# The two full attention layers of a four-layer kernel: scores issued in runs of three pairs, value products behind them, and the operands of the next quad loaded across block borders

## The chip, the cores and the metric

The kernel runs on one core of one Trainium2 chip. The metric is the device time of one execution in microseconds. Before the change it is 2768.49 us (median of three runs, 2767.56 to 2770.2).

## The reference

Four attention layers follow one another on x of 2048 rows by 512 columns (one batch): a window layer (each query sees itself and the 255 keys before it), a full layer, a window layer and a full layer. Each has 32 heads of 16 columns.

```python
x = x + _A_ref(_layernorm(x), A_wqkv, A_wo)      # window layer
x = x + _B_ref(_layernorm(x), B_wqkv, B_wo)      # full layer
x = x + _A_ref(_layernorm(x), A_wqkv, A_wo)
x = x + _B_ref(_layernorm(x), B_wqkv, B_wo)

def _B_ref(x, wqkv, wo):                         # B, S, D = 1, 2048, 512; H = 32; Dh = 16
    qkv = (x @ wqkv).reshape(B, S, 3, H, Dh).transpose(2, 0, 3, 1, 4)
    q, k, v = qkv[0], qkv[1], qkv[2]
    p = softmax(einsum("bhqd,bhkd->bhqk", q, k) * Dh ** -0.5)     # no mask: all 2048 keys
    o = einsum("bhqk,bhkd->bhqd", p, v)
    return o.transpose(0, 2, 1, 3).reshape(B, S, D) @ wo
```

The change is about the two calls of `_B_ref`, layers 1 and 3 (counted from 0).

## The kernel before, in words

**Units of the full layers.** The 2048 queries are cut into four blocks c of 512, the heads into eight quads qd of four, the keys into sixteen tiles j of 128. Layer 1 goes through c, then qd, then j. Layer 3 goes through t (pairs of quads), then c, then the two quads of t, then j. Each layer so has 32 quads in all, 512 key tiles and 1024 *pairs*: a pair is two heads of one key tile.

**A pair** (`exps`, L706 to L719): TensorE makes two score products of 128 keys by 512 queries (L714) into one score tile, and ScalarE takes the exponential of the whole tile, 128 by 1024 (L718), into a buffer e. There are three score tiles in a full layer: two of the pool `ps_s` (L198) and a third one made by `phase` (L408). They are used in turn (L709), so the scores of pair p overwrite what the exponential of pair p-3 reads. There are six e buffers (`EB`, L34).

**The values of a key tile** (`pv` in `attn_full`, L756 to L760): four products of 17 value columns, one for each head, added up in `acc[0]` over the sixteen tiles. They read the two e buffers of the tile. When a quad is done, `epilogue` (L678) has VectorE move `acc[0]` out and divide by the sums; the values of the next quad go to the same `acc[0]`.

**Side work.** Projections, output products and normalisation of other blocks and layers are generators (`Work`, L799). In full layers they hand out one *piece* at a time: four matmuls of 32 output columns over 512 (or 256) columns (`mms`, L427 to L430), which the program counts as 0.222 us (`MM`, L32). Twelve pieces make a group in most of them, three in `wo_part`. All groups of a full layer are added up in the one bank `acc[1]` (L412 to L413), which must be read out before the next group starts; `mms` notes the time from which that is so in `PH["free"]` (L438). `Side` (L860) doles the pieces out: `step` (L908) is called once for each key tile, `share` (L924) gives out pieces by a budget, and `finish` (L935) issues all that is left. In layer 1 there are two `Side` objects (the first half of block 0, then the rest of the layer), in layer 3 one for each of the sixteen blocks (t, c).

**Order.** TensorE's order is that of the program as written (`manual_schedule`, L203); a planned clock (`clock`, `spent`) only decides which side work is handed out where. In `attention` (L955), for each key tile of a full layer: scores of both pairs, then the values of the tile two before (`flush(2)`, L984), then side work (`sd.step()`, L985). So TensorE's order is S S V X, S S V X, with S the scores of a pair, V the values of a key tile, and X side work of zero to several pieces.

**Operands.** `load_full` (L727) loads the queries of a quad (two buffers) and its keys in two halves (three buffers) over SyncE's DMA queue. `attention` calls it for the next quad of the same block at the start of a quad (L977), and for the first quad of a block at the start of the block (L972), behind `sd.finish()` and `settle()` of the block before (L991 and L993). `settle` (L587) issues the small products that are still open after key and query projections.

Of the kernel before, what the change touches and what calls it, by code (L numbers as in the profile page):

```python
# [19 lines left out]
P = 128  # L20
NT = S // P
# [165 lines left out]
def fast_path(ctx, tc, flag, a_x, a_wqkv, a_wo, b_wqkv, b_wo, out):  # L187
# [25 lines left out]
    def spent(us):  # L213
        clock[0] += us
        return us
# [161 lines left out]
    def share(ty):  # L377

        s = vp.tile([P, NHT], F32, name=f"sh{ty}", tag="sh")
        h = vp.tile([P, NHT], F32, name=f"sg{ty}", tag="sh")  # L380
        q, k = (es[:, ty, i, :].bitcast(I32) for i in (0, 1))
        s, h = s.bitcast(I32), h.bitcast(I32)
        nc.vector.tensor_scalar(s, q, 1, None, op0=ALU.logical_shift_right)
        nc.vector.tensor_scalar(h, k, 1, None, op0=ALU.logical_shift_right)
        nc.vector.tensor_tensor(s, s, h, ALU.add)
        nc.vector.tensor_scalar(k, s, 0x7F800000, None, op0=ALU.bitwise_and)
        nc.vector.tensor_tensor(s, s, k, ALU.subtract)
        nc.vector.tensor_tensor(h, s, s, ALU.add)
        nc.vector.tensor_tensor(q, k, h, ALU.add)
# [197 lines left out]
    def settle(all_=True):  # L587
        while pend and (all_ or pend[0][0] <= clock[0]):
            pend.pop(0)[1]()
# [116 lines left out]
    def exps(name, kt, qt, pr, pieces):  # L706

        turn["s"] += 1
        ps = PH["third"] if PH["full"] and turn["s"] % 3 == 0 else ps_s.tile([P, 2, QC], F32, name=f"s{name}", tag="s")  # L709
        w0 = min(p[3] for p in pieces)  # L710
        w1 = max(p[3] + p[2] for p in pieces)
        for kc, qc, wd_, s0 in pieces:
            for h in range(2):
                nc.tensor.matmul(ps[:, h, s0:s0 + wd_], kt[R * h:R * h + R, pr, kc:kc + P],  # L714
                                 qt[R * h:R * h + R, pr, qc:qc + wd_], start=True, stop=True)
        spent(0.27)
        e = pp.tile([P, 2, QC], F32, name=f"e{name}", tag="e", bufs=EB)
        nc.scalar.activation(e[:, :, w0:w1], ps[:, :, w0:w1], AF.Exp, scale=SCALE)  # L718
        return e  # L719

    def flush(n):
        while len(pvq) > n:
            spent(1.0)
            for f in pvq.popleft():
                f()
# [21 lines left out]
            nc.sync.dma_start(kt[:, :, :WIN], kw[c - 1][pair, :, QC - WIN:].rearrange("r p n -> p r n"))  # L747
        return kt, qt

    def attn_full(l, c, qd, kt, qt, a):  # L750
        for j in range(NT):
            es_ = []
            for pr in range(2):
                es_.append(exps(f"{l}_{c}_{qd}_{j}_{pr}", kt[j // 8], qt, pr, [(j % 8 * P, 0, QC, 0)]))

            def pv(j=j, es_=es_):  # L756
                for h in range(4):
                    nc.tensor.matmul(a[32 * h:32 * h + DH + 1, :], V[l, qd // 4, j // 8][:, j % 8, 4 * (qd % 4) + h, :],  # L758
                                     es_[h // 2][:, h % 2, :], start=(j == 0), stop=(j == NT - 1),
                                     skip_group_check=True)  # L760
            yield pv

# [95 lines left out]
    class Side:  # L860

        def __init__(self, steps, works=(), following=(), least=0.0):
            self.next, self.least = list(following), least
            self.q, self.steps, self.cost, self.spent, self.k = [], steps, 0.0, 0.0, 0
            self.budget = self.lag = 0.0
            for w in carried:
                self.add(w)
            carried.clear()
            for w in works:
                self.add(w)  # L870
# [5 lines left out]
        def one(self, force=False):  # L876

            if force:
                self.prefetch()
            at = [(w.ready_at(), i) for i, w in enumerate(self.q)]  # L880
            at = [(r, i) for r, i in at if r is not None]
            now = [i for r, i in at if r <= clock[0]]
            if now:
                i = now[0]
            elif force:
                r, i = min(at)
                clock[0] = r
            else:
                return None
            return self.piece(self.q[i])  # L890

        def piece(self, w):
            c = w.advance()
            if c is None:
                self.q.remove(w)
                return 0.0
            self.spent += abs(c)
            return c

        def prefetch(self):  # L900
# [4 lines left out]
                if any(w.w and not w.open for w in part):  # L905
                    break

        def step(self):  # L908
            self.k += 1
            self.prefetch()  # L910

            for w in list(self.q):
                r = w.ready_at() if w.aside else None
                if r is not None and r <= clock[0]:
                    self.piece(w)
            if PH["full"]:
                return self.share()
            s0, due = self.spent, self.cost * self.k / (self.steps - 2)
            while self.q and self.spent < due and self.spent - s0 < 3:
                c = self.one()  # L920
                if c is None or c < 0 and self.spent - s0 >= 2 and due - self.spent < 4:
                    break

        def share(self):  # L924

            self.budget = min(self.budget + max((self.cost - self.spent) / max(self.steps - 3 - self.k, 1), self.least), 0.75)
            self.lag = max(self.lag - max(0.29, self.least), -0.3)
            while self.q and clock[0] >= PH["free"] and self.budget >= MM / 2 and (self.lag < 0.25 or self.budget > 0.45):
                c = self.one()
                if c is None:  # L930
                    break
                self.budget -= abs(c)
                self.lag += abs(c)

        def finish(self):  # L935

# [7 lines left out]
    def run(g):  # L944
        for _ in g:
            pass
# [5 lines left out]
    pvq = deque()  # L952
    PK, PV, PO = 48 * MM + 0.3, 48 * MM, 48 * MM

    def attention(l, works):  # L955

        win = l % 2 == 0
        phase(l)
        load = load_win if win else load_full
        sd = None  # L960
        for t in range(NHT if l == 3 else 1):
            for c in range(NQ):
                qds = range(2 * t, 2 * t + 2) if l == 3 else range(NQD)
                if l == 1:

                    sd = sd or Side(NT * NQD // 2, works[0], works[1], 0.33)
                    while ("Q", 1, c) not in DONE:
                        sd.one(True)
                    settle()
                else:  # L970
                    sd = Side((3 if win else NT) * len(qds), works[t * NQ + c], works[t * NQ + c + 1], 0.34 if l == 3 and t < 2 else 0.0)
                ops = load(l, c, qds[0])  # L972
                for qd in qds:
                    if (l, c, qd) == (1, 0, NQD // 2):
                        sd.finish()
                        sd = Side(NT * NQD * NQ - NT * NQD // 2, works[1], works[2], 0.33)
                    nxt = load(l, c, qd + 1) if qd + 1 in qds else None  # L977
                    a = acc[qd % 2 if win else 0]
                    began = clock[0]
                    for f in (attn_win if win else attn_full)(l, c, qd, *ops, a):  # L980
                        clock[0] = max(clock[0], began + (2.4 if win else 1.8))
                        began = clock[0]
                        pvq.append([f])
                        flush(2)  # L984
                        sd.step()  # L985
                        if win:
                            settle(False)
                    pvq[-1].append(lambda l=l, c=c, qd=qd, a=a: epilogue(l, c, qd, a))
                    ops = nxt
                if l != 1 or c == NQ - 1:  # L990
                    sd.finish()  # L991
                if not win:
                    settle()  # L993
        flush(0)
        phase(None)

    def T(l, c):
# [15 lines left out]
    def shift3(ht):  # L1013
        def gen():
            key_shift(3, ht)
            yield -1e-6
        return Work(gen(), 0.0, None, [("K3", c, ht) for c in range(NQ)])

    def O3(c, ht):
        return Work(wo_part(c, ht), PO / 4, None, [("O", 3, c, ht)], True)  # L1020
# [21 lines left out]
    def all_of(works, following=()):  # L1042
        Side(1, works, following).finish()
# [102 lines left out]
    lasts = {0: [VV(1, 3)], 2: [VV(3, 3, True, (0,))]}  # L1146
    for l in range(4):
        if l % 2 == 0:
            attention(l, works[l] + [tails[l]])
            all_of(tails[l], lasts[l])  # L1150
            key_shift(l + 1, 0 if l else None)
            all_of(lasts[l], works[l + 1][0])
        else:
            attention(l, works[l] + [works[2][0] if l == 1 else [O3(3, 3)]])
    all_of([O3(3, 3)])


# [37 lines left out]
```

## Time and profile before

| what | us |
|---|---|
| median of three runs | 2768.49 |
| profiled execution | 2767.5 |
| its span, first to last instruction | 2765.8 |
| TensorE matmul busy | 2629.3 |
| ScalarE busy | 2377.9 |
| VectorE busy | 959.7 |
| GpSimd busy | 567.7 |

The profiled execution took 2767.5 us, of which 2765.8 us lie between its first and its last instruction. Busy times are sums over the whole span; the stages have different limits, so they are to be read stage by stage. Layer 1 takes about the stretch from 507 to 1458 us, layer 3 that from 1792 to 2748 us of the span. In the profile a line such as "L714 PE MATMUL s<-qt,kt" is TensorE's score product, "L758" the value product, "L429" (and L550) side work of the full layers, and "L718 ACT" the exponential. A busy TensorE is not a TensorE at its peak, since matmuls overlap.

### The profile page before, as it was taken

To read this page: it belongs to the slowest core of one execution; us is meant where nothing else is said; L and a number is where in the kernel's file an instruction comes from. 1 tells how busy PE (TensorE), PEld (TensorE's weight loads), DVE (VectorE), ACT (ScalarE), POOL (GpSimd) and SP (SyncE) were. 2 spreads that over 40 slices of the span, in tenths; PEclk is the share of its full clock that TensorE was granted. 3 is DMA by queue.
4 is the path that set the end of the run, shared out by engine and by line. 5 is a ranking of instruction groups with operands and counts; after the bars stand their busy time and mean duration, and the time that the engine had idled before them with its cause. 6 is when DMAs were issued, how large, how long until landed. Compare 5 with 4: busy or idle time off the path is not lost.

```text
span 2765.8 us, 59954 instructions
## 1 busy us (share of the span) xinstructions
PE 2629.3 (95%) x24502; PEld 779.9 (28%) x24502; DVE 959.7 (35%) x2063; ACT 2377.9 (86%) x2683; POOL 567.7 (21%) x1129
## 2 busy tenths in 40 slices
PE   8989989999999999999998888899999999999997
PEld 4333334322222222222223333422222222222221
DVE  7678765112131113112215676512222222222122
ACT  3666655799999999999995677399999999999997
POOL 2577662000000000000005677100000000000000
PEclk9999999999999999999999999999999999999999
DMA  7877775422232123212325564623333343333331
GB/s 225 224 244 227 224 202 161 139 70 89 85 100 88 63 81 108 85 60 91 101 68 177 149 186 133 177 66 112 105 117 116 120 124 104 102 107 114 99 96 56
DMA packets 318542, 345.32 MB, mean 125 GB/s; under 512 B 113072, under 2 KB 234416, under 8 KB 312240
## 3 DMA queue, kind: packets, MB, share of 16 engines
q1 hardware_dynamic: 318256, 341.39, 41.0%
q8 instruction: 194, 3.18, 0.5%
q14 instruction: 92, 0.75, 0.1%
HBM read 228.59 MB, written 96.99 MB: 118 GB/s over the span
## 4 chain that ended last, share of the span: by engine, by line
PE 74%; ACT 8%; issue 6%; DVE 6%; POOL 3%; DMA 3%; SPq 0%; ACTq 0%; DVEq 0%; POOLq 0%
PE acc L758 30%; PE s L714 19%; PE acc L429 10%; PE b L432 9%; ACT e L718 7%; PE acc L791 3%; PE bs L432 1%; POOL e L781 1%; POOL e L784 1%; DVE ot L686 1%; POOL wr L344 1%; DMA w<-wd 1%; DVE xh L469 1%; DVE sp L528 0%; DVE xn L463 0%
## 5 line engine op out<-in xcount | busy, mean ns | idle before, releaser
L718 ACT ACTIVATE e<-s 128x1024 f32<-128x1024 f32 (+2 forms) x2432 | 2245.6, 1115 | 106.4 <-PE s L714 98.4
L758 PE MATMUL acc<-e,vt 128*17 128x512 f32 x8192 | 1078.8, 598 | 4.9 <-DVE ot L686 4.1
L714 PE MATMUL s<-qt,kt 64*128 64x512 f16 (+3 forms) x5504 | 777.8, 355 | 68.2 <-ACT e L718 40.0
L714 PEld LDWEIGHTS <-kt 64*128 64x128 f16 x5504 | 203.1, 94 | 807.4 <-issue 776.0
L784 POOL TENSOR_SCALAR_AFFINE_SELECT e<-e 128x256 f32<-128x256 f32 x512 | 230.4, 457 | 116.0 <-ACT e L718 115.3
L758 PEld LDWEIGHTS acc<-e,vt 128*17 128x17 f32 x8192 | 136.2, 95 | 383.6 <-issue 351.8
L686 DVE STREAM_TRANSPOSE ot<-acc 128x512 f32<-128x512 f32 x128 | 91.3, 714 | 374.6 <-PE acc L758 308.5
L781 POOL TENSOR_SCALAR_AFFINE_SELECT e<-e 128x256 f32<-128x256 f32 x448 | 196.8, 445 | 91.0 <-ACT e L718 89.5
L702 POOL TENSOR_TENSOR oh<-o,oh 128x512 f16<-128x512 f32 x31 | 36.0, 1161 | 860.2 <-DVE oh L701 860.2
L791 PE MATMUL acc<-e,vt 128*17 128x384 f32 (+2 forms) x2816 | 202.0, 393 | 6.1 <-POOL e L781 4.0
L432 PE MATMUL b<-xc,w 128*128 128x512 f16 x684 | 159.4, 384 | 16.8 <-DMA w<-wd 7.8
L533 POOL TENSOR_TENSOR sq_h<-sp_h 128x512 bf16<-128x512 f16 x27 | 28.1, 1041 | 510.8 <-DVE sp_h L527 510.8
L525 ACT ACTIVATE sp<-b,es 128x512 f16<-128x512 f32 x57 | 39.2, 688 | 96.0 <-PE b L432 93.7
L527 DVE TENSOR_SCALAR sp<-acc,es 128x512 f16<-128x512 f32 x28 | 20.9, 748 | 288.9 <-PE acc L429 288.9
L638 DVE COPY vt<-acc 128x256 f32<-128x256 f32 (+1 forms) x40 | 20.2, 504 | 288.9 <-PE acc L429 288.9
L527 DVE TENSOR_SCALAR sp_h<-acc,es 128x512 f16<-128x512 f32 x27 | 20.3, 751 | 277.8 <-PE acc L429 277.1
L533 POOL TENSOR_TENSOR sq<-sp 128x512 bf16<-128x512 f16 x28 | 29.1, 1041 | 396.9 <-DVE sp L527 396.9
L429 PE MATMUL acc<-xc,w_h 128*32 128x512 f16 x1296 | 108.1, 379 | 2.3 <-DVE km L566 2.3
L429 PE MATMUL acc<-xc,w 128*32 128x512 f16 x1344 | 108.9, 379 | 0.3
L673 DVE TENSOR_TENSOR dx<-acc,gcol 128x512 f32<-128x512 f32 x60 | 41.5, 692 | 176.7 <-PE acc L429 176.7
L429 PE MATMUL acc<-wv,xc 128*32 128x256 f16 (+1 forms) x1920 | 101.7, 306 | 0.0
L429 PE MATMUL acc<-wo,oh 128*32 128x512 f16 x1296 | 101.3, 379 | 0.0
(167 smaller groups left out, 1767.0 us busy)
## 6 DMA issues: line engine op xcount, KB each, us to landing
kt<-kf SPq DMA_DIRECT2D x128, 512.0 KB
qt<-qs SPq DMA_DIRECT2D x128, 256.0 KB
xd<-x SPq DMA_DIRECT2D x96, 256.0 KB
x<-xd SPq DMA_DIRECT2D x96, 256.0 KB
w<-wd SPq DMA_DIRECT2D x20, 1024.0 KB
kt<-kw SPq DMA_DIRECT2D x64, 256.0 KB
qs<-sp SPq DMA_DIRECT2D x48, 256.0 KB
wo<-wd SPq DMA_DIRECT2D x12, 1024.0 KB
```

The costliest lines, as they stand in the source:

```text
L429: nc.tensor.matmul(ps[g:g + 32], a[:, g:g + 32], b, start=(i == 0), stop=(i == len(pairs) - 1), skip_group_check=True)
L432: nc.tensor.matmul(ps, a, b, start=(i == 0), stop=(i == len(pairs) - 1))
L527: nc.vector.tensor_scalar(sp[:, 0], ps, e, None, op0=ALU.mult)
L533: nc.gpsimd.tensor_tensor(sq, sp[:, 0], sp[:, 0], ALU.mult)
L673: nc.vector.tensor_tensor(d, ps, gcol[1], ALU.mult)
L686: nc.vector.transpose(ot.rearrange("p b r -> p (b r)"), a)
L714: nc.tensor.matmul(ps[:, h, s0:s0 + wd_], kt[R * h:R * h + R, pr, kc:kc + P], qt[R * h:R * h + R, pr, qc:qc + wd_], start=True, stop=True)
L718: nc.scalar.activation(e[:, :, w0:w1], ps[:, :, w0:w1], AF.Exp, scale=SCALE)
L758: nc.tensor.matmul(a[32 * h:32 * h + DH + 1, :], V[l, qd // 4, j // 8][:, j % 8, 4 * (qd % 4) + h, :], es_[h // 2][:, h % 2, :], start=(j ...
L781: nc.gpsimd.affine_select(v, v, pattern=[[0, 2], [-1, P]], compare_op=ALU.is_gt, fill=0.0, base=0, channel_multiplier=1)
L784: nc.gpsimd.affine_select(v, v, pattern=[[0, 2], [1, P]], compare_op=ALU.is_ge, fill=0.0, base=0, channel_multiplier=-1)
L791: nc.tensor.matmul(a[32 * h:32 * h + DH + 1, q * P:(q + nb) * P], V[l, (4 * c + j) // 4][:, j % 4, 4 * qd + h, :], es_[h // 2][:, h % 2, s ...
```

## The change

In the full layers TensorE's order becomes runs of three pairs: the scores of three pairs (one and a half key tiles, without regard to quad borders), then the values of at most two key tiles that were complete at the end of the run before, then side work. A run in which the output of a quad is finished (`epilogue`) takes no values behind it. `Side.step` gets a `room`: 1.79 us less 0.87 us for each key tile's values in this run, but at least one piece, or two where a quad ends. The old brake `lag` goes; the cap of the budget is six pieces (1.332 us), and the least income is 0.65 us for a run in place of 0.33 or 0.34 us for a key tile. Side work that has begun a group goes on with it (`within`). The operands of the next quad are loaded in the second half of a quad, also over the border of a block, once the works that make them are done; if they are not, they are loaded at the start of the quad as before. The window layers get a function of their own, with the old loop.

```diff
-    def attn_full(l, c, qd, kt, qt, a):
...
+    def values_of(l, c, qd, j, es_):
+
+        def pv():
+            spent(0.87)
+            for h in range(4):
+                nc.tensor.matmul(acc[0][32 * h:32 * h + DH + 1, :], V[l, qd // 4, j // 8][:, j % 8, 4 * (qd % 4) + h, :],
+                                 es_[h // 2][:, h % 2, :], start=(j == 0), stop=(j == NT - 1), skip_group_check=True)
+        return pv
...
+            if self.within and self.within in self.q:
+                return self.piece(self.within)
...
+            self.within = w if PH["full"] and c > 0 else None
             return c
...
-        def share(self):
-
-            self.budget = min(self.budget + max((self.cost - self.spent) / max(self.steps - 3 - self.k, 1), self.least), 0.75)
-            self.lag = max(self.lag - max(0.29, self.least), -0.3)
-            while self.q and clock[0] >= PH["free"] and self.budget >= MM / 2 and (self.lag < 0.25 or self.budget > 0.45):
+        def share(self, room):
+
+            self.budget = min(self.budget + max((self.cost - self.spent) / max(self.steps - 2 - self.k, 1), self.least), 6 * MM)
+            while self.q and clock[0] >= PH["free"] and self.budget >= MM / 2 and room >= MM / 2:
                 c = self.one()
                 if c is None:
                     break
                 self.budget -= abs(c)
-                self.lag += abs(c)
+                room -= abs(c)
...
+    def attention_full(l, works):
...
+        runs = lambda n: n * 2 * NT // 3
+        sd, ops, block = None, None, -1
+        pairs, began, ready, due = 0, clock[0], [], deque()
+
+        def upcoming(i):
+
+            t, c, qd = quads[i]
+            if l == 1:
+                return [("Q", 1, c)]
+            return [("Q3", c, t), ("S3", t)] + [("K3", k, t) for k in range(NQ)]
+
+        def emit(all_=False):
+            n, over = 0, False
+            while due:
+                f = due[0]
+                if f.__name__ == "pv":
+                    if not all_ and (n == 2 or over):
+                        break
+                    n += 1
+                else:
+                    over = True
+                due.popleft()()
+            return n, over
+
+        def run():
+
+            nonlocal pairs, began
+            pairs = 0
+            spent(0.22)
+            n, over = emit()
+            due.extend(ready)
+            ready.clear()
+            sd.step(max(1.79 - 0.87 * n, 2 * MM if over else MM))
+            clock[0] = began = max(clock[0], began + 2.71)
+
+        for i, (t, c, qd) in enumerate(quads):
+            if l == 1 and qd == 0 or l == 3 and qd % 2 == 0:
+                if l == 3:
+                    if sd:
+                        sd.finish()
+                    b = t * NQ + c
+                    sd = Side(runs(2), works[b], works[b + 1], 0.65 if t < 2 else 0.0)
+                else:
+
+                    sd = sd or Side(runs(NQD // 2), works[0], works[1], 0.65)
                     while ("Q", 1, c) not in DONE:
                         sd.one(True)
...
+            elif (l, c, qd) == (1, 0, NQD // 2):
+                sd.finish()
+                sd = Side(runs(NQD * NQ - NQD // 2), works[1], works[2], 0.65)
+            kt, qt = ops or load_full(l, c, qd)
+            ops = None
+            for j in range(NT):
+                es_ = []
+                for pr in range(2):
+                    es_.append(exps(f"{l}_{c}_{qd}_{j}_{pr}", kt[j // 8], qt, pr, [(j % 8 * P, 0, QC, 0)]))
+                    if pr:
+                        ready.append(values_of(l, c, qd, j, es_))
+                        if j == NT - 1:
+                            ready.append(lambda c=c, qd=qd: epilogue(l, c, qd, acc[0]))
+                    pairs += 1
+                    if pairs == 3:
+                        run()
+                        if j >= NT // 2 and not ops and i + 1 < len(quads) and all(d in DONE for d in upcoming(i + 1)):
                             settle(False)
...
+                            if not pend:
+                                ops = load_full(l, *quads[i + 1][1:])
+        due.extend(ready)
+        sd.finish()
+        settle()
+        emit(True)
         phase(None)
```

More of the change, by code (lines that the diff above doesn't have):

```diff
@@ L748, in load_win @@
         return kt, qt
-    def attn_full(l, c, qd, kt, qt, a):
[L751 to L761, printed above, removed]
+    def values_of(l, c, qd, j, es_):
[5 more added lines that the diff above has]
+        return pv
     WTILES = (((-2, 0, 1, 0), (1, 1, 3, 1)), ((-1, 0, 2, 0), (2, 2, 2, 2)), ((0, 0, 3, 0), (3, 3, 1, 3)))
@@ L864, in __init__ @@
             self.q, self.steps, self.cost, self.spent, self.k = [], steps, 0.0, 0.0, 0
-            self.budget = self.lag = 0.0
+            self.budget = 0.0
+            self.within = None
             for w in carried:
@@ L906, in prefetch, with step @@
                     break
-        def step(self):
+        def step(self, room=0.0):
             self.k += 1
@@ L916, in step @@
             if PH["full"]:
-                return self.share()
+                return self.share(room)
             s0, due = self.spent, self.cost * self.k / (self.steps - 2)
@@ L953, in fast_path, with attention_win @@
     PK, PV, PO = 48 * MM + 0.3, 48 * MM, 48 * MM
-    def attention(l, works):
-        win = l % 2 == 0
+    def attention_win(l, works):
         phase(l)
[L959 to L966, printed above, removed]
+        for c in range(NQ):
+            sd = Side(3 * NQD, works[c], works[c + 1])
+            ops = load_win(l, c, 0)
+            for qd in range(NQD):
+                nxt = load_win(l, c, qd + 1) if qd + 1 < NQD else None
+                a = acc[qd % 2]
+                began = clock[0]
+                for f in attn_win(l, c, qd, *ops, a):
+                    clock[0] = max(clock[0], began + 2.4)
+                    began = clock[0]
+                    pvq.append([f])
+                    flush(2)
+                    sd.step()
+                    settle(False)
+                pvq[-1].append(lambda c=c, qd=qd, a=a: epilogue(l, c, qd, a))
+                ops = nxt
+            sd.finish()
+        flush(0)
+        phase(None)
@@ new lines, in attention_full @@
+    def attention_full(l, works):
+        phase(l)
+        quads = [(t, c, qd) for t in range(NHT if l == 3 else 1) for c in range(NQ)
+                 for qd in (range(2 * t, 2 * t + 2) if l == 3 else range(NQD))]
+        runs = lambda n: n * 2 * NT // 3
[36 more added lines that the diff above has]
+                    sd = sd or Side(runs(NQD // 2), works[0], works[1], 0.65)
@@ L967, in attention @@
                     while ("Q", 1, c) not in DONE:
                         sd.one(True)
[L969 to L986, printed above, removed]
-                            settle(False)
-                    pvq[-1].append(lambda l=l, c=c, qd=qd, a=a: epilogue(l, c, qd, a))
-                    ops = nxt
@@ L990, in attention @@
[L990 to L994, printed above, removed]
+                settle()
[16 more added lines that the diff above has]
+                        if j >= NT // 2 and not ops and i + 1 < len(quads) and all(d in DONE for d in upcoming(i + 1)):
+                            settle(False)
+                            if not pend:
+                                ops = load_full(l, *quads[i + 1][1:])
@@ L995, in attention @@
+        due.extend(ready)
+        sd.finish()
+        settle()
+        emit(True)
         phase(None)
@@ L1016, in gen @@
             yield -1e-6
-        return Work(gen(), 0.0, None, [("K3", c, ht) for c in range(NQ)])
+        return Work(gen(), 0.0, ("S3", ht), [("K3", c, ht) for c in range(NQ)])
     def O3(c, ht):
@@ L1148, in fast_path @@
         if l % 2 == 0:
-            attention(l, works[l] + [tails[l]])
+            attention_win(l, works[l] + [tails[l]])
             all_of(tails[l], lasts[l])
             key_shift(l + 1, 0 if l else None)
+            DONE["S3", 0] = clock[0]
             all_of(lasts[l], works[l + 1][0])
         else:
-            attention(l, works[l] + [works[2][0] if l == 1 else [O3(3, 3)]])
+            attention_full(l, works[l] + [works[2][0] if l == 1 else [O3(3, 3)]])
     all_of([O3(3, 3)])
```

## The prediction

> **What bounds the kernel now.** First the page, for the span; then the instructions of layer 1 (507 to 1460 us) and layer 3 (1792 to 2750 us) grouped by line.
>
> ```profile
> span 2765.8 us, 59954 instructions
> PE 2629.3 (95%) x24502; PEld 779.9 (28%) x24502; DVE 959.7 (35%) x2063; ACT 2377.9 (86%) x2683; POOL 567.7 (21%) x1129
> ...
> L718 ACT ACTIVATE e<-s 128x1024 f32<-128x1024 f32 x1024 | 947.1, 1084 | 3.7 <-PE s L714 2.7
> ...
> L718 ACT ACTIVATE e<-s 128x1024 f32<-128x1024 f32 x1024 | 946.7, 1199 | 14.4 <-PE s L714 13.5
> ```
>
> The exponentials fill ScalarE in both layers: 1024 in each, hardly any idle time before them. The timeline gives their pace and the ends of each layer:
>
> ```profile
> 699.22 13.88 ACT L718 ACTIVATE e<-s 128x1024 f32<-128x1024 f32 x15
> 507.05 7.45 ACT L718 ACTIVATE e<-s 128x1024 f32<-128x1024 f32 x8
> 1456.78 1.09 ACT L718 ACTIVATE e<-s 128x1024 f32<-128x1024 f32 x1
> 1792.42 1.02 ACT L718 ACTIVATE e<-s 128x1024 f32<-128x1024 f32 x1 [5.96 <-PE s L714]
> 2745.84 1.71 ACT L718 ACTIVATE e<-s 128x1024 f32<-128x1024 f32 x1
> ```
>
> A single one takes about 1.02 us (fourth row), but fifteen in a row take 13.88, so the next ends (13.88 - 1.04) / 14 = 0.917 us after the one before. At that pace 1024 need 1.02 + 1023 x 0.917 = 939.1 us. Layer 1 takes 507.05 to 1457.87, 950.8 us, and layer 3 takes 1792.42 to 2747.55, 955.1 us. So **ScalarE is the bound, and 11.7 + 16.0 = 28 us is all that any order of TensorE can win in the two layers.**
>
> Where the 28 us go, and TensorE's costs, is read from a stretch of its timeline:
>
> ```profile
> 660.53 0.61 PE L429 MATMUL acc<-xc,w 128*32 128x512 f16 x8
> 661.08 0.61 PE L714 MATMUL s<-qt,kt 64*128 64x512 f16 x4
> 661.62 1.05 PE L758 MATMUL acc<-e,vt 128*17 128x512 f32 x8
> 662.49 0.40 PE L429 MATMUL acc<-xc,w 128*32 128x512 f16 x4
> 662.82 0.61 PE L714 MATMUL s<-qt,kt 64*128 64x512 f16 x4
> ...
> 669.00 1.05 PE L758 MATMUL acc<-e,vt 128*17 128x512 f32 x8
> 669.98 0.39 PE L714 MATMUL s<-qt,kt 64*128 64x512 f16 x2
> ```
>
> From start to start: scores of two pairs to values 0.54; values of a tile to side work 0.87; two pieces (x8) to the next scores 0.55, one piece (x4) 0.33, so 0.22 a piece; values straight to scores 0.98. A key tile with two pieces takes 0.54 + 0.87 + 0.55 = 1.96 us, over ScalarE's 2 x 0.917 = 1.83; with one it takes 1.74. Tiles alternate between one and two, 1.85 on average: TensorE falls behind by a few hundredths for each tile, by 0.12 where two pieces follow two.
>
> **The order and its price.** No product, exponential or DMA is added or removed; only TensorE's order, and the place of the operand loads, change. A run of three pairs needs ScalarE for 3 x 0.917 = 2.75 us. What the run saves: the changes scores-values and side work-scores come 341 times in a layer in place of 512. Each cycle has about 0.10 + 0.11 us of them (0.54 less two pairs at 0.22; 0.33 less 0.22), so 171 x 0.21 = 36 us less TensorE time in each layer. The Trainium skill ("TensorEngine Tiling (Array Packing)", Key Properties) says that changing the tiling mode drains the engine. By that rule alone the new order wins; the rows show the same price of a change (and none from values to side work, 0.87 against 0.86 for values to values), but as time of an engine that is not the bound, and that case is rival (1).
>
> What it adds is **a wait of the third pair's scores.** There are three score tiles used in turn, so pair p cannot be written before the exponential of pair p-3 has ended. In the old order a run of two pairs leaves one tile spare, and in layer 1 the scores waited for ScalarE once:
>
> ```profile
> PE s L714 <- ACT e L718: 0.5, 1, 0.5
> ...
> 507.95 1.04 ACT L718 ACTIVATE e<-s 128x1024 f32<-128x1024 f32 x1
> 508.85 1.06 ACT L718 ACTIVATE e<-s 128x1024 f32<-128x1024 f32 x1
> 509.96 0.39 PE L714 MATMUL s<-qt,kt 64*128 64x512 f16 x2 [0.53 <-ACT e L718]
> 510.28 1.05 PE L758 MATMUL acc<-e,vt 128*17 128x512 f32 x8
> ```
>
> That one case shows the price. The exponential ends at 508.85 + 1.06 = 509.91, the waiting scores start 0.05 later, and the values behind them start at 510.28, 0.32 after the scores, though the exponentials that they read had ended by 507.95 + 1.04 = 508.99: nothing behind a waiting matmul passes it. In a run of three, the third pair waits for the third exponential of the run before. Let that end at E. From E ScalarE has three exponentials left, and the first one after them is on time if it ends by E + 4 x 0.917 = E + 3.67. How long before that its scores must start:
>
> ```profile
> 2006.19 0.61 PE L714 MATMUL s<-qt,kt 64*128 64x512 f16 x4
> 2006.68 1.02 ACT L718 ACTIVATE e<-s 128x1024 f32<-128x1024 f32 x1 [1.42 <-PE s L714]
> ...
> 1458.28 0.33 PEld L758 LDWEIGHTS acc<-e,vt 128*17 128x17 f32 x8
> 1458.49 1.90 PE L758 MATMUL acc<-e,vt 128*17 128x512 f32 x16
> 1458.93 0.12 PEld L758 LDWEIGHTS acc<-e,vt 128*17 128x17 f32 x4 [0.31 <-issue]
> 1459.36 0.12 PEld L758 LDWEIGHTS acc<-e,vt 128*17 128x17 f32 x4 [0.31 <-issue]
> ```
>
> Start of the scores to end of the exponential is 0.49 + 1.02 = 1.51. Values behind values step by 0.43 for half a tile, 0.86 for a tile. So the next run's scores must start by E + 2.16, and before them stand 0.05 + 0.32 and then the run's values and side work: **these may take 1.79 us.** A run with two tiles and one piece takes 0.86 + 0.87 + 0.33 = 2.06: late by 0.27. Without a piece it takes 0.86 + 0.98 = 1.84: late by 0.05. A run with one tile and four pieces takes 0.87 + 3 x 0.22 + 0.33 = 1.86, but behind a late run its third pair no longer waits, so it costs nothing and makes up the rest; then its successor's third pair waits again. The sum of two runs (2 x 0.75 for six pairs, plus 2.06 and 1.86) is 5.42, under ScalarE's 5.50: TensorE has the time, but a wait of some 0.37 in every second run takes it away.
>
> How often: runs and key tiles stand three to two, so one and two tiles alternate. Walking the rule through the code, a layer has 341 runs; a two-tile run begins 160 times behind a shorter one, 150 of these alone and 10 followed by another. A two-tile run gets one piece whenever side work is ready (room one `MM`). Of the 150, 140 cost 0.27, and 10, which end a quad, get two pieces and cost 0.49. In the 10 doubles the end of a quad has put off a key tile's values by a run, and the second exponential waits for the e buffer: the values end at about E + 0.37 + 1.05, the exponential so at E + 2.44 in place of 1.83, 0.61 late, and the second run adds 0.27. That is 37.8 + 4.9 + 8.8 = 51.5 us a layer; some 13 runs in layer 1 and 10 in layer 3 find no side work, less 0.22 each: **98 us in both.** Nearest bounds: 0.05 for all 320, 16 us; 0.27 and more for all, 103.
>
> **Side work that does not fit.** One and four pieces alternate, but a group's end stops the run's pieces (`PH["free"]`), so twelve pieces go as 1, 4, 1, 4, 1, 1: six runs, two pieces a run.
>
> ```profile
> L429 PE MATMUL acc<-xc,w 128*32 128x512 f16 x1344 | 108.9, 379 | 0.3
> L429 PE MATMUL acc<-wv,xc 128*32 128x256 f16 (+1 forms) x1152 | 70.0, 326 | 0.0
> L429 PE MATMUL acc<-wo,oh 128*32 128x512 f16 x576 | 46.4, 379 | 0.0
> ...
> L528 DVE SCALAR_TENSOR_TENSOR sp<-acc,es,sp 128x512 f16<-128x512 f32 x28 | 21.0, 751 | 0.9
> L527 DVE TENSOR_SCALAR sp<-acc,es 128x512 f16<-128x512 f32 x28 | 20.9, 748 | 288.9 <-PE acc L429 288.9
> ...
> 1458.72 0.69 DVE L638 COPY vt<-acc 128x512 f32<-128x512 f32 x1 [7.98 <-PE acc L429]
> ```
>
> Layer 1 has 3072 / 48 = 64 groups: 12 half-width ones in the first `Side`, which fit, and 52 in the second, 312 runs where 299 are; and three times nothing is ready for some 8 runs between an output block and the projections that need its normalisation. Some 7 groups are left for `finish`, with ScalarE idle: three of keys, 12 x 0.22 + two readouts of 0.75 + 0.4 = 4.5 each, four of values, 2.6 + 0.69 + 0.3 = 3.6 each; 28 less a lead of 2: **26 us.** In layer 3 a block of t < 2 has about 26 runs' work in 21: two groups of `wo_part`, some 2.3 us with readouts, are forced at the border, of which 1.8 show, seven times, and about 5 us in the later blocks: **18 us.** Bounds: nothing if the groups fit, and twice these.
>
> **Operands.** The loads keep their number; they stand later in their quad, half a quad (over 13 us) ahead of use, and no longer behind a block's last side work. Layer 3's first load bounds a missed one:
>
> ```profile
> 1787.86 19.10 SPq L735 DMA_DIRECT2D kt<-kf  x2
> 1791.71 1.46 PE L714 MATMUL s<-qt,kt 64*128 64x512 f16 x6 [5.67 <-DMA kt<-kf]
> ```
>
> Scores start 3.9 us after it is issued. I take it as covered; what it can win at borders is in the 28 us, and three missed at the borders of t would cost 12. The window layers' code does the same as before: nothing.
>
> **The sum.** 2767.5 (the profiled execution) - 28 + 98 + 26 + 18 = 2881.5; the median stands 1 us above that execution: **2882 us**, 4% slower.
>
> **Rivals.**
> (1) *TensorE had been the bound, and the spared changes free it*: both layers run at 939 us, 2768 - 28 = 2740. For it: the X8 tiles over 1.83, and the total of 5.42 under 5.50. It needs the third pair's wait not to bind: from values and side work of at most 1.79 in every run on, and two tiles alone take 1.84. 0.09.
> (2) *Two-tile runs seldom get a piece* (the planned clock holds work back): 320 x 0.05 = 16 in place of 98, and 0 to 20 of forced work: 2756 to 2776. 0.09, a third of it on each side of no change.
> (3) *Late runs as worked out, but the side work fits*: 2882 - 44 = 2838. 0.18.
> (4) *TensorE's clock falls*, since it now stops shortly in every second run.
>
> ```profile
> 1700.00:1800.00 100.00, 84.11 (x765) 43.09 (x767) 57.95 (x126) 47.74 (x64) 36.20 (x84) 0.93 0.57 158
> 2300.00:2400.00 100.00, 99.15 (x905) 24.06 (x903) 26.99 (x53) 100.00 (x110) 4.51 (x5) 1.00 0.38 116
> ```
>
> Full layers had a granted clock of 1.00; at 84% busy, between layers, it was 0.93. At 0.93 the 2.38 us before the next scores grow by 0.17, 320 times: 2882 + 54 = 2936. 0.04. The Trainium skill ("TensorE: Matmul & The Clock Gate", A second HAM failure mode: psum-queue depth-cycling) says that short idle spells between groups of matmuls can make the gate swing; no run here shows that at this scale.
>
> The forecast itself has 0.60. Faster by over 0.2% (about what a measurement here can tell from no change): 0.09 + 0.03 = 0.12; within: 0.03; slower: 0.85. The range leaves out (1) and (2): from 2800 (half the two-tile runs late, little forced) to 2940 (more forced, or the clock).
>
> **What would show it.** Scores (L714) waiting for ScalarE (L718) some 170 times in each layer, 50 us or more; in a two-tile run 0.37 + 2.06 us from the third pair's scores to the next run's scores; exponentials idle by about 0.27 once in six; a burst of side work at the end of layer 1. If the scores wait but the exponentials keep their pace, 1.79 is wrong; if they do not wait at all, the argument falls.

## The result and the profile after

| | us |
|---|---|
| before, median of 4 runs | 2768.02 (2766.88 to 2770.2) |
| after, median of 4 runs | 2895.47 (2891.85 to 2899.36) |
| ratio | 1.046, 95% interval 1.044 to 1.0479 |
| profiled execution before, after | 2767.5, 2899.36 |

The change makes the kernel 4.6% slower. The page of the changed kernel gives the same work over a longer span (the value products now stand on line 755):

```profile
span 2897.6 us, 59956 instructions
PE 2618.6 (90%) x24502; PEld 873.2 (30%) x24502; DVE 959.4 (33%) x2063; ACT 2397.6 (83%) x2683; POOL 567.1 (20%) x1129
```

Where the 131.8 us between the two spans came from is read from the first and the last exponential of each full layer in the timeline:

```profile
508.96 1.03 ACT L718 ACTIVATE e<-s 128x1024 f32<-128x1024 f32 x1
1497.65 1.02 ACT L718 ACTIVATE e<-s 128x1024 f32<-128x1024 f32 x1 [0.17 <-PE s L714]
1855.63 1.02 ACT L718 ACTIVATE e<-s 128x1024 f32<-128x1024 f32 x1 [6.54 <-PE s L714]
2877.41 1.02 ACT L718 ACTIVATE e<-s 128x1024 f32<-128x1024 f32 x1
```

| stretch | before | after | more |
|---|---|---|---|
| up to layer 1's first exponential | 507.05 | 508.96 | 1.9 |
| layer 1's exponentials | 950.8 | 989.7 | 38.9 |
| from there to layer 3's first | 334.6 | 357.0 | 22.4 |
| layer 3's exponentials | 955.1 | 1022.8 | 67.7 |
| rest of the span | 18.2 | 19.2 | 1.0 |

Nearly all of it lies in the two layers and right behind layer 1. ScalarE's pace of 939.1 us for a layer is the measure for what follows: layer 1 is now 50.6 us over it (11.7 before), layer 3 is 83.7 over (16.0). I call this the *surplus* of a layer.

The groups and the waits of layer 1, then of layer 3, show what the exponentials wait for. A row of waits gives the total, how often, and the longest:

```profile
L718 ACT ACTIVATE e<-s 128x1024 f32<-128x1024 f32 x1024 | 956.5, 1039 | 33.2 <-PE s L714 27.5 <-PE acc L755 5.7
...
PE s L714 <- ACT e L718: 63.0, 194, 0.5
ACT e L718 <- PE s L714: 27.5, 146, 0.4
ACT e L718 <- PE acc L755: 5.7, 10, 0.6
...
PE s L714 <- ACT e L718: 73.5, 191, 0.5
ACT e L718 <- PE s L714: 56.5, 141, 6.5
```

Scores waited for an exponential once in layer 1 before; now they do so 194 times, and the exponentials wait in turn 146 times for scores and 10 times for values, which hold an e buffer. Both engines wait for each other: TensorE stands still for 63 us in all, though its scores come late 146 times. Two runs, one after the other, in the timeline of layer 1:

```profile
1196.28 5.60 ACT L718 ACTIVATE e<-s 128x1024 f32<-128x1024 f32 x6 [0.17 <-PE s L714]
1196.54 1.05 PE L755 MATMUL acc<-e,vt 128*17 128x512 f32 x8
1197.41 1.05 PE L429 MATMUL acc<-xc,w 128*32 128x512 f16 x16
1198.38 0.60 PE L714 MATMUL s<-qt,kt 64*128 64x512 f16 x4
1199.18 0.39 PE L714 MATMUL s<-qt,kt 64*128 64x512 f16 x2 [0.19 <-ACT e L718]
1199.51 1.91 PE L755 MATMUL acc<-e,vt 128*17 128x512 f32 x16
1201.23 0.40 PE L429 MATMUL acc<-xc,w 128*32 128x512 f16 x4
1201.56 0.82 PE L714 MATMUL s<-qt,kt 64*128 64x512 f16 x6
1202.06 5.61 ACT L718 ACTIVATE e<-s 128x1024 f32<-128x1024 f32 x6 [0.17 <-PE s L714]
```

The third pair's scores (x2, at 1199.18) wait 0.19 for the exponential that reads their tile. Only then come two tiles of values, one piece, and the next run's scores at 1201.56, 2.38 us later. Six exponentials take 1202.06 - 1196.28 = 5.78 us in place of 5.50. The idle time shown is 0.17 and not 0.28, since an exponential that is not late shows its start some 0.1 before the end of the one before.

Behind layer 1 stands what side work is left, with ScalarE idle:

```profile
1499.52 2.77 PE L429 MATMUL acc<-xc,w 128*32 128x512 f16 x48 [1.64 <-DVE sp L528]
1503.99 0.71 PE L550 MATMUL acc<-sq,hsum 128*32 128x512 bf16 x4 [1.70 <-DVE sp L528]
1505.48 2.77 PE L429 MATMUL acc<-wv,xc 128*32 128x512 f16 x48 [0.78 <-DVE km L566]
1509.05 2.77 PE L429 MATMUL acc<-wv,xc 128*32 128x512 f16 x48 [0.79 <-DVE vt L638]
...
1518.77 1.90 PE L755 MATMUL acc<-e,vt 128*17 128x512 f32 x16
```

Each group of twelve pieces (x48) takes 2.77 us, and TensorE then waits 0.79 (values) or 1.64 (keys) until VectorE has read out the one bank. Five such groups lengthen the time from the last exponential of layer 1 to the next layer's first scores from 2.5 us (1457.87 to 1460.33) to 21.9 (1498.67 to 1520.60), by 19.5 of the 22.4 us in the table. The other 2.9 lie between there and layer 3, where the mean granted clock was 0.98 in place of 0.99. The same happens in small at the borders of the blocks of layer 3, here at the one with the longest wait:

```profile
2110.76 0.83 PE L429 MATMUL acc<-wo,oh 128*32 128x512 f16 x12 [0.45 <-DMA qs<-sp_h]
2112.39 0.83 PE L429 MATMUL acc<-wo,oh 128*32 128x512 f16 x12 [0.79 <-DVE dx L673]
2114.01 0.83 PE L429 MATMUL acc<-wo,oh 128*32 128x512 f16 x12 [0.79 <-DVE dx L673]
2115.63 0.83 PE L429 MATMUL acc<-wo,oh 128*32 128x512 f16 x12 [0.79 <-DVE dx L673]
2117.01 0.61 PE L714 MATMUL s<-qt,kt 64*128 64x512 f16 x4 [0.55 <-DMA qt<-qs]
```

Four groups of `wo_part`, 1.62 us apart, stand ahead of the next block's scores. Added up over the trace (each exponential's end against 0.917 us after the end of the one before), seven such borders cost 29.8 us of layer 3's 83.7.

### The profile page after: what moved, and what is told of

It reads as the page before. It is cut to its first block, busy times and chain, and to the rows that moved or that the text cites. A ratio compares the mean times of both kernels' runs of the same rounds, so it can differ in the third digit from the quotient of the medians.

```text
span 2897.6 us, 59956 instructions
## 1 busy us (share of the span) xinstructions
PE 2618.6 (90%) x24502; PEld 873.2 (30%) x24502; DVE 959.4 (33%) x2063; ACT 2397.6 (83%) x2683; POOL 567.1 (20%) x1129
## 4 chain that ended last, share of the span: by engine, by line
PE 54%; ACT 25%; issue 9%; DVE 5%; POOL 3%; DMA 2%; SPq 0%; ACTq 0%; POOLq 0%; DVEq 0%
ACT e L718 24%; PE acc L755 22%; PE s L714 15%; PE b L432 9%; PE acc L429 4%; PE acc L787 3%; PE bs L432 1%; POOL e L777 1%; POOL e L780 1%; POOL wr L344 1%; DVE xh L469 0%; DVE dx L673 0%; DMA w<-wd 0%; DVE xn L463 0%; DVE xh L463 0%
## 5 line engine op out<-in xcount | busy, mean ns | idle before, releaser
L755 PE MATMUL acc<-e,vt 128*17 128x512 f32 x8192 | 1012.6, 596 | 0.1
L714 PEld LDWEIGHTS <-kt 64*128 64x128 f16 x5504 | 260.4, 94 | 894.7 <-issue 800.7
L755 PEld LDWEIGHTS acc<-e,vt 128*17 128x17 f32 x8192 | 170.6, 96 | 388.9 <-issue 375.4
L432 PEld LDWEIGHTS <-w 128*128 128x128 f16 x720 | 68.1, 99 | 114.9 <-issue 36.2
L429 PE MATMUL acc<-xc,w 128*32 128x512 f16 x1344 | 101.0, 379 | 1.6 <-DVE sp L528 1.6
L429 PE MATMUL acc<-xc,w_h 128*32 128x512 f16 x1296 | 98.9, 379 | 2.3 <-DVE km L566 2.3
L429 PE MATMUL acc<-wv,xc 128*32 128x256 f16 (+1 forms) x1920 | 92.4, 306 | 3.2 <-DVE vt L638 2.4
```

Source lines behind the costliest of these rows:

```text
L429: nc.tensor.matmul(ps[g:g + 32], a[:, g:g + 32], b, start=(i == 0), stop=(i == len(pairs) - 1), skip_group_check=True)
L432: nc.tensor.matmul(ps, a, b, start=(i == 0), stop=(i == len(pairs) - 1))
L755: nc.tensor.matmul(acc[0][32 * h:32 * h + DH + 1, :], V[l, qd // 4, j // 8][:, j % 8, 4 * (qd % 4) + h, :], es_[h // 2][:, h % 2, :], star ...
```

## The experiments

The theory: a run of three pairs fills all three score tiles, so the third pair holds TensorE until an exponential ends, and from there values and side work may take 1.79 us; two-tile runs take more. The rivals: TensorE's total time counts; runs of three are slow whatever stands in them; forced side work is the main cost. Each experiment is read in layer 1, from its first and last exponential, where little side work is forced.

**No piece in a two-tile run.**

```diff
-            sd.step(max(1.79 - 0.87 * n, 2 * MM if over else MM))
+            sd.step(max(1.79 - 0.87 * n, 0.0))
```

> Changed kernel, but a run with two key tiles' values gets no piece of side work (no least piece). Read in layer 1, whose 1024 exponentials take 989.7 us in the changed kernel, 50.6 more than 939.1. Theory of the wait (third pair's scores held by the exponential of the run before, so that values and side work of each run may take 1.79 us): a two-tile run drops from 2.06 to 1.84 us, is late by 0.05 in place of 0.27, and the surplus of layer 1 falls to about 15 us (169 x 0.05 and ten waits for an e buffer of 0.6). More is then left for the forced end: 97 pieces behind layer 1 in place of 62 (some 12 us more), 16 to 20 at seven borders of layer 3 in place of 6 to 12 (some 25 us more there). In all about 2860 to 2880. Rival, runs of three are slow whatever stands in them (e buffers, or the number of scores in a row): the surplus of layer 1 stays near 50 and the time goes up by the forced work, over 2920.

Measured: 2933.11 us, ratio to before 1.0598 (1.0579 to 1.0618). Layer 1's exponentials, and the waits there:

```profile
507.09 1.03 ACT L718 ACTIVATE e<-s 128x1024 f32<-128x1024 f32 x1
1465.05 1.02 ACT L718 ACTIVATE e<-s 128x1024 f32<-128x1024 f32 x1
...
ACT e L718 <- PE acc L755: 8.0, 11, 2.1
ACT e L718 <- PE s L714: 0.2, 1, 0.2
```

They take 959.0 us, a surplus of 19.9 in place of 50.6 (about 15 expected): the theory holds where it is asked, and runs of three are not slow in themselves. One wait of 2.1 us, at forced work halfway through the first block, is about half of the difference from 15. The total missed what the theory gave (2860 to 2880), and it even passed the rival's 2920. The reason lies in the forced work. The stretch from layer 1 to layer 3 is 20.4 us longer than after (12 expected):

```profile
1471.92 5.17 PE L429 MATMUL acc<-xc,w 128*32 128x512 f16 x48 [6.97 <-DMA xc<-xh]
...
1493.52 4.46 PE L429 MATMUL acc<-wv,xc 128*32 128x512 f16 x48 [0.78 <-DVE km L566]
```

The 36 more pieces are three groups of keys, at 4.4 each some 13 us, near what was expected. But the first group waits 6.97 us for a transfer of its input, and two groups take 5.17 and 4.46 in place of 2.77, at a granted clock of 0.88 from 1466 to 1510 us. And at seven borders of layer 3 the trace loses 12 to 14 us each, 88.3 in place of 29.8. One of them:

```profile
2043.97 0.38 PE L550 MATMUL acc<-sq_h,hsum 128*32 128x512 bf16 x1 [2.02 <-POOL sq_h L533]
2046.74 1.42 PE L429 MATMUL acc<-wo,oh 128*32 128x512 f16 x12 [0.79 <-DVE dx L673]
2048.94 1.47 PE L429 MATMUL acc<-wo,oh 128*32 128x512 f16 x12 [0.79 <-DVE dx L673]
2051.20 1.47 PE L429 MATMUL acc<-wo,oh 128*32 128x512 f16 x12 [0.79 <-DVE dx L673]
2054.00 3.41 PE L755 MATMUL acc<-e,vt 128*17 128x512 f32 x16
```

A group now takes 1.42 to 1.47 in place of 0.83, two tiles of values 3.41 in place of 1.9: beside the longer list, the clock fell (see the last section). My expectation had priced the pieces, and neither the clock nor the wait for input. How the loss at the borders divides between the longer list and the clock was not measured.

**The third pair's scores behind the first tile of values.** When two pairs of a run are out, the first tile's values are issued, then the third pair.

```diff
...
+                    if pairs == 2:
+                        first[:] = emit(False, 1)
                     es_.append(exps(
...
             n, over = emit()
+            n, over = n + first[0], over or first[1]
```

> Changed kernel, but the third pair's scores stand behind the run's first key tile of values: S S V S V X in place of S S S V V X, with the same side work in each run. It adds two changes between scores and values in each run, 341 x 0.21 = 72 us of TensorE time in each layer. Theory of the wait: the third pair no longer has to wait for the exponential of the run before, so TensorE can work ahead; it is then limited by its own time, three double runs of a group of twelve pieces take 16.9 us against 16.5 of ScalarE, and the surplus of layer 1 falls from 50.6 to about 27 us; with layer 3 alike, about 2850. Rival, TensorE's total time is what counts: both layers get slower by up to 70 us each, 2950 or more.

Measured: 2855.09 us, ratio 1.0316 (1.0298 to 1.0335), 40 us less than the changed kernel. Layer 1:

```profile
509.24 1.03 ACT L718 ACTIVATE e<-s 128x1024 f32<-128x1024 f32 x1
1479.60 1.02 ACT L718 ACTIVATE e<-s 128x1024 f32<-128x1024 f32 x1 [0.19 <-PE s L714]
...
PE s L714 <- ACT e L718: 10.4, 23, 0.5
ACT e L718 <- PE s L714: 14.3, 70, 0.4
...
1203.16 1.05 PE L755 MATMUL acc<-e,vt 128*17 128x512 f32 x8
1204.15 0.39 PE L714 MATMUL s<-qt,kt 64*128 64x512 f16 x2
1204.47 1.05 PE L755 MATMUL acc<-e,vt 128*17 128x512 f32 x8
```

The surplus is 971.4 - 939.1 = 32.3 us (27 expected), with scores waiting 23 times in place of 194. The last rows show what was added: values to scores 0.99 and scores to values 0.32, where the values of two tiles stood 0.86 apart. So more TensorE work in each run, at the right place, made both layers faster (layer 3's exponentials take 996.6 us in place of 1022.8). This is the clearest evidence against TensorE's total time as the bound.

**Two pieces in every run.**

```diff
-            sd.step(max(1.79 - 0.87 * n, 2 * MM if over else MM))
+            sd.step(max(1.79 - 0.87 * n, 2 * MM))
```

> Changed kernel, but every run gets at least two pieces of room, so a two-tile run may take two pieces. Theory of the wait: a two-tile run with two pieces is late by 0.49 in place of 0.27; there are 117 of them in layer 1 and 46 two-tile runs without side work (0.05), so the surplus of layer 1 rises from 50.6 to about 63 us; but all side work fits, so the forced end behind layer 1 (about 20 us) and the forced work at the borders of layer 3 (about 25 us) go. In all 2865 to 2885. Rival, forced side work is the main cost and pieces in two-tile runs are nearly free as long as two runs together need less than 5.5 us: the surplus of layer 1 stays at 50 or less, and the time falls by 40 us or more, below 2855.

Measured: 2884.09 us, ratio 1.0421 (1.0402 to 1.044). Layer 1:

```profile
506.95 1.03 ACT L718 ACTIVATE e<-s 128x1024 f32<-128x1024 f32 x1
1511.67 1.02 ACT L718 ACTIVATE e<-s 128x1024 f32<-128x1024 f32 x1
```

The surplus rises to 1005.7 - 939.1 = 66.6 us (63 expected), while no border of layer 3 holds the exponentials for over 1.7 us, and the stretch behind layer 1 is back to 333.6 us. With the run without pieces, this gives the price step by step: a two-tile run with no piece, one or two delays the exponentials by 0.05, 0.27 to 0.28 and about 0.5 us each. Forced work was not the main cost, but it costs more than a piece in a run: 19.5 us for some 60 pieces behind layer 1 of the changed kernel is 0.32 each, against 0.22.

**The kernel before with two score tiles.** The old order, but no spare tile.

```diff
-        ps = PH["third"] if PH["full"] and turn["s"] % 3 == 0 else ps_s.tile([P, 2, QC], F32, name=f"s{name}", tag="s")
+        ps = ps_s.tile([P, 2, QC], F32, name=f"s{name}", tag="s")
```

> Kernel before (runs of two pairs), with two score tiles in place of three, so that the second pair's scores wait for the exponential of the pair two before: no spare tile, as in the changed kernel, but with the old order and the old side work. Theory (what costs is that a run fills all the score tiles): values and side work of a run may then take 0.87 us (3 x 0.917 less 0.05, 0.32 and 1.51) and take 0.98 without a piece, 1.20 with one, 1.42 with two, so a run behind a waiting one is late by 0.11, 0.33 or 0.55, and one behind a late run makes it up. With about 187 runs of two pieces, some of them in a row, and about 70 of two and a half or more or of one piece behind one, the surplus of layer 1 over 939.1 us rises from 12 to 110 to 140 us, with layer 3 alike: 2960 to 3020 in all, with some hundreds of waits of scores for exponentials. Rival, three pairs' scores in a row are the cause (their length on TensorE or the six e buffers): the surplus stays under 20 us and the time near 2769.

Measured: 3003.48 us, ratio 1.0849 (1.0818 to 1.0881). Layer 1:

```profile
508.58 1.03 ACT L718 ACTIVATE e<-s 128x1024 f32<-128x1024 f32 x1
1582.63 1.02 ACT L718 ACTIVATE e<-s 128x1024 f32<-128x1024 f32 x1
...
ACT e L718 <- PE s L714: 99.8, 218, 1.1
PE s L714 <- ACT e L718: 78.5, 215, 0.5
```

The surplus goes from 11.7 to 136.0 us (110 to 140 expected). The old order, with neither runs of three nor other side work, shows the same pair of waits once the spare tile is gone. So it is the lost spare tile that costs, not the three pairs.

**The kernel before with the new loading of operands alone.** The loads for the next quad move to the second half of a quad, across block borders.

```diff
...
-                    nxt = load(l, c, qd + 1) if qd + 1 in qds else None
+                    nxt = load(l, c, qd + 1) if win and qd + 1 in qds else None
...
+                        elif j >= NT // 2 and not nxt and i < len(quads) and all(d in DONE for d in upcoming(i)):
+                            settle(False)
+                            if not pend:
+                                nxt = load_full(l, *quads[i][1:])
...
```

> Kernel before, with only the loading of operands changed: the next quad's queries and keys are loaded in the second half of a quad, across block borders, once they are made. Theory: in the kernel before hardly any scores wait for these loads (once, 5.7 us, at the start of layer 3, which stays), so the time stays within 3 us of the kernel before. Rival, the early loads are worth something at the borders (layer 3 has about 9 us of short delays there): 5 to 9 us faster.

Measured: 2768.76 us against 2768.87 for the kernel before on the same chip, ratio 0.9999 (0.999 to 1.0009). In the old order this part of the change shows no effect, within some 2.6 us either way.

A seventh e buffer, which would show the ten waits for values by themselves, was not tried. None of these versions beats the kernel before.

## Why the prediction was right

The forecast was 2882 us, in a range of 2800 to 2940; the median is 2895.47. By its steps:

- **ScalarE as the bound, 28 us to win at most.** Not contradicted: no kernel of this study brought a layer to 939.1 us; layer 1 comes closest in the old order (950.8 us, and 950.7 with the new loading of operands). That none could win more was not tested.
- **The third pair's wait and 1.79 us.** Held: 2.38 us from the third pair's scores to the next run's scores were forecast for a two-tile run with one piece (0.32 + 2.06), and 2.38 are in the timeline. (The prediction's list of signs has 0.37 + 2.06 there; 0.05 of the 0.37 lies ahead of these scores.) In layer 1, 138 exponentials end 0.2 to 0.3 us late, 38.8 us in all (forecast: 140, and the second runs of the 10 doubles, less the 13 without side work, so 137 times 0.27, 37.0), and 19 by 0.45 to 0.8, 11.2 us (forecast: 10 ends of quads at 0.49 and 10 waits for an e buffer at 0.61, 11.0).
- **98 us for both layers.** The surplus of layer 1 is 50.6 (48.6 by the sum). That of layer 3 without its seven borders is 83.7 - 29.8 = 53.9; the layer's start and one wait some 25 us ahead of each of the three borders of t, which cost before too, are 6.1 of these, which leaves 47.8 (49.3 by the sum).
- **26 us behind layer 1.** 22.4, of which forced work is 19.5. A group was sized right (2.77 + 0.79 = 3.6, and 4.5 for keys); five groups were left, not seven. So 2.9 us of the agreement are luck: the sum had nothing for them.
- **18 us at the borders of layer 3.** 29.8, the term that was mis-sized: I counted two groups of `wo_part` forced at a border, 1.8 us shown seven times; the order has 6 to 12 pieces, two to four groups at 1.62 us, and a border costs 1.8 to 6.2 us. The 5 us for the later blocks did not show. With the 6.1 us of the point before last, which the sum had taken as won (it counted all 28 us as gone), this makes up most of the 18 us by which the profiled execution came out over the 2881.5 of the sum.
- **Operands and window layers at nothing.** Held; the first by an experiment of its own in the old order, and in the changed kernel layer 3's scores wait for these loads only at its start, as before, and for 0.55 us at the border shown.
- **Rivals.** (1), the spared changes free TensorE: the time per change was right (values to scores 0.99, scores to values 0.32), but the changes that were added with the third pair's scores behind the first values made both layers faster, so it is not what bounds. (2), pieces seldom given: in the timeline 150 of 169 two-tile runs of layer 1 have side work, and 131 of 170 of layer 3. (3), the side work fits: it did not. (4), the clock: over each of the two layers of the changed kernel the mean granted clock is 1.00, in spite of a wait in every second run; it did fall at the forced work of the kernel without pieces.

## What to carry to other kernels

An engine that issues in order must not fill all the buffers of its consumer in one go: from the last of them on, its next start is tied to the consumer's end, and what stands in between has a hard limit for each run, whatever the average leaves free. Before runs are made longer to save changes of mode, compare the longest run, not the mean, with the time from the release of the last buffer to the next result that the bound engine needs. Side work that no longer fits comes back at a border, in the open, at a higher price.

## What the runs showed of the hardware

TensorE's clock halved where its work became sparse, and that I had not expected at these gaps. The stretches at the border of the experiment without pieces (columns: stretch and its length, busy time of TensorE, its weight loads, VectorE, ScalarE and GpSimd, then granted clock, DMA share and GB/s):

```profile
2042.00:2044.00 2.00, 0.03 (x1) 0.12 (x2) 1.50 (x2) 0.00 (x0) 1.04 (x1) 1.00 0.68 225
2044.00:2046.00 2.00, 1.17 (x13) 0.39 (x13) 0.69 (x2) 0.00 (x0) 0.00 (x0) 1.00 0.89 258
2046.00:2047.50 1.50, 0.76 (x9) 0.34 (x12) 1.38 (x2) 0.00 (x0) 0.00 (x0) 0.78 0.59 205
...
2051.00:2053.00 2.00, 1.80 (x14) 0.45 (x15) 1.12 (x3) 0.00 (x0) 0.00 (x0) 0.50 0.65 214
```

One wait of 2.02 us, then groups with waits of about 0.8, and from about 2047 us on the clock is 0.50 for some 10 us, and a border cost about 12 us or more, where the changed kernel's cost 2 to 6. At the changed kernel's border above, the same waits of 0.79 between groups, without the long one, left it at 1.00:

```profile
2112.00:2118.00 6.00, 3.48 (x46) 1.15 (x47) 5.17 (x8) 0.49 (x1) 0.00 (x0) 1.00 0.77 248
```

The busy share tells the two apart. From 2042 to 2046 us, ahead of the fall, TensorE is busy for 1.20 of 4.00 us; in the row above for 3.48 of 6.00. The seven traces together show it as a pattern. Every spell at 0.50 that begins and ends inside a span lasts 3.4, 6.8, 10.2 or 13.7 us, so the clock goes by windows of 3.41 us. Of the windows at 1.00, 81 were followed by a fall, and TensorE was busy for at most 0.52 of them; every window under 0.43 was followed by a fall, and between 0.43 and 0.52 both occur. Back at 1.00 it came only after windows at 0.50 that were busy for 0.84 or more (74 times), never after 0.83 or less (49 times). So a fall lasts until TensorE is nearly full again. That is a pattern of these traces, with modelled ends of matmuls; no run varied the busy share on purpose. The Trainium skill ("TensorE: Matmul & The Clock Gate", Part 1: The HAM clock gate) gives the two states as full and half rate, which the 0.50 agrees with, and names an idle window of about 3.4 us for the fall; here no single wait in the stretch was longer than 2.02 us.
